# v loaded in fp32 and cast by GpSimd, two half sums moved to DMA, and a new order of steps, in a gated linear attention with a rational MLP

## The chip, the cores and the metric

One Trainium2 chip, one NeuronCore. The time is device microseconds of one execution; the number for a kernel is the median of its runs. The engines are TensorE (PE, with its weight loads as PEld), VectorE (DVE), ScalarE (ACT), GpSimd (POOL) and SyncE (SP, which here only issues DMAs).

## The reference

Inputs `q`, `k`, `v`, `f_logit` are fp32 of shape (4 batches, 8 heads, 768 tokens, 48); `w_in` is 384x2048, `w_out` 2048x384.

```
f = 1 / (1 + exp(-f_logit))
for t in tokens:                                  # per batch and head
    state = f[t][:, None] * state + outer(k[t], v[t])      # 48 x 48
    y[t]  = q[t] @ state
x = y as 3072 tokens x 384
h = x @ w_in
P = a0 + a1*h + a2*h^2 + a3*h^3
Q = 1 + |b0|*|h| + |b1|*h^2
out = (P / (Q + 1e-6)) @ w_out                    # fp32, 3072 x 384
```

## The kernel before, in words

**Units.** The work is cut into 12 units of 256 tokens: unit n is chunk n // 4 of batch n % 4, so units n and n + 4 share a state. Of a unit's 256 tokens partition p holds tokens 2p and 2p + 1, and the upper and lower 64 partitions are two blocks j of 128 tokens. All in a unit is one chain of steps, and each step is one function of the kernel that issues a few instructions:

- `ld` (line 193) loads f, k, q or v of the unit. f, k and q go through SP's queue as fp32 into tiles with three buffers each. v goes through POOL's queue, whose DMA casts it to bf16, also with three buffers.
- `ef`, `ls` (271, 276, ACT) make log(1 + exp(-f)); `cs` (286, PE) sums it along the tokens; `A` (302, ACT) are the exponentials; `xa` (308, DVE) multiplies k (`xa n 1`) and q (`xa n 0`) by them; `T` (320, PE) transposes and `Te` (330, 332) copies out.
- `sc` (345, PE) makes the scores, `mk` (353, DVE) multiplies them by the causal mask into `scm`. `kv` (414, PE) makes the new part of the state from k and **v**, `si` (425) adds the old state, `ae`, `st` (441, 445) scale it.
- `yi`, `yb` (367, PE) sum y from the old state and from scores times v. A head is 48 wide and PE writes y in pieces of 32, so a pair of heads makes three pieces: the first and last read **v** as loaded; the middle one, which lies across both heads, reads `vmp`, a tile that `vm` (360, POOL) fills with two copies of 16 columns per pair of heads: two POOL instructions of 128 elements per partition in each unit.
- `ye` (435, 436) copies y out as xT. `h` (454; `ha`, `hb` 478) multiplies by w_in in four pieces of four 128-column blocks; `hy` (484, ACT) copies out.
- The rational function: `sq` (489) makes h^2, `ab` (497) |h|; Q is summed by PE (`u`, 505), by DVE (`zv`, 515) or by an accumulating DMA from POOL's queue (`zd`, 519); ACT makes 1/Q as exp(-ln Q) (`ln` 510, `lz` 523, `ex` 527). `p1` (531), `pm` (545), `p2` (536) make the two halves of P on DVE, which are summed by DVE (`tv`, 553) or by an accumulating DMA (`ta`, 549); `gm` (557, DVE) multiplies by 1/Q. A **half sum** is `zv`, `zd`, `tv` or `ta` on 8 of the 16 blocks (2048 elements per partition).
- `o` (567, PE) multiplies by w_out, `oe` (574) copies out, `so` (580) stores.
- `wi` (199) and `wo` (205) load w_in and w_out in four parts each by POOL's queue with a cast. `dz` (295) are matmuls that only keep PE busy.

**Order.** The text `ORDER` lists 823 steps, and each engine runs its own instructions in the order in which the steps stand there (`tc.manual_schedule()`); waits between engines follow from the data and the buffers. So the order of two steps matters when they share an engine or a DMA queue. `>ls.1` behind a step makes it wait for that other step, `@2` names the PSUM slot. PSUM has four slots that all steps share.

Of the kernel before, what the change touches and what calls it, by code (L numbers as in the profile page):

```python
# [8 lines left out]
F32 = mybir.dt.float32  # L9
# [10 lines left out]
ld 0 f 2 4; cu 1; cz 0; ab_ b a; ld 0 f 0 2; cz 2; ld 0 k 0 2; cu 0; ld 0 k 2 4; ld 0 q 2 4; ci; cm; dz 9 @0  # L20
ld 0 q 0 2; ld 1 f; ld 0 v; ab_ a s; ld 1 k; fa; ld 1 q; ef 0 2 4; ef 0 0 2; cz 3; ls 0 0 2; ls 0 2 4; cz 1
cs 0 2 4 @2; cs 0 0 2 @3; A 0 0 2 4; dz 4 @0; A 0 1 2 4; xa 0 0 2 4; A 0 1 0 2; xa 0 1 2 4; A 0 0 0 2
xa 0 1 0 2; T 0 2 4 @0; vm 0 1; kv 0 @3; Te 0 2 4; wi 8 12; xa 0 0 0 2; ae 0; sc 0 1 @0; si 0 0; mk 0 1
T 0 0 2 @2; ef 1; dz 5 @1; fr; Te 0 0 2; ld 2 f >mk.0.1; ls 1; ld 3 f; st 0 0; sc 0 0 @0; ld 2 k; cs 1 @2
wi 12 16 >ls.1; mk 0 0; ld 2 q; ld 3 k; yi 0 1 @1; vm 0 0; A 1 1; ld 1 v; ld 3 q; yb 0 2 4; yb 0 0 2; A 1 0
si 0 1; wi 4 8; ye 0 0 1 v; ye 0 1 3 s; xa 1 1; wi 0 4; h 0 8 12 @1; xa 1 0; ld 2 v; fb; T 1 @0; hy 0 8 12 v
Te 1 s; st 0 1; ab 0 8 12; ha 0 12 16 @0; ef 2; sc 1 1 @3; sc 1 0 @1; mk 1 1; ls 2; hb 0 12 16; cs 2 @2; ld 5 f
sq 0 8 12; hy 0 12 16; ld 4 f; mk 1 0; kv 1 @3; vm 1 1; ld 4 q; vm 1 0; A 2 1; si 1 0; dz 1 @0; ae 1; A 2 0
yb 1 0 2 @1; st 1 0; yb 1 2 4; sq 0 12 16; yi 1 1; si 1 1; p1 0 8 16; ye 1 s; h 0 4 8 @2; ab 0 12 16; ef 3
pm 0 8 16; h 1 12 16 @1; ls 3; st 1 1; hy 0 4 8; p2 0 8 16; h 1 8 12 @0; hy 1 12 16; ab 0 4 8; sq 0 4 8  # L30
h 0 0 4 @2; hy 1 8 12; xa 2 1; ab 1 8 16; h 1 4 8 @3; ld 5 k; hy 0 0 4; ld 4 k; sq 1 8 16; ld 6 f; cs 3 @1
# [12 lines left out]
h 3 4 8 @1; ef 7; pm 2 0 16; hy 3 8 12; o 0 1 4 8; hy 3 4 8; sc 4 1 @0; o 0 1 0 4; ls 6; mk 4 1; ta 2 8 16
sc 4 0 @1; ex 1 0 8; o 0 0 0 4; ld 9 f; xa 5 0; cs 6 @0; mk 4 0; o 0 0 4 8; A 6 1; o 0 0 12 16; st 4 0; A 6 0
yb 4 0 2 @1; ab 3 0 16; yb 4 2 4; oe 0 0 2 s; yi 4 0; yi 4 1; si 4 1; sq 3 0 16; ye 4 s; T 5 @2; ef 8
u 2 0 4 @1; Te 5 s; h 4 4 8 @0; st 4 1; zd 3 8 16; ln 2 0 4; gm 1 8 16; h 4 12 16 @2; lz 2 8 16; p1 3 0 16
sc 5 0 @3; h 4 0 4 @1; xa 6 0; hy 4 4 8; vm 6 1; ta 2 0 8; gm 1 0 8; hy 4 12 16; ld 9 q; h 4 8 12 @0; vm 5 0
ld 7 k; ld 7 v; hy 4 0 4; mk 5 0; vm 6 0; u 2 4 8 @2; zd 3 0 8; hy 4 8 12; pm 3 0 16; o 1 1 4 8 @1; ln 2 4 8
o 1 0 0 4; ex 2 8 16; sc 5 1 @2; kv 5 @0; mk 5 1; yi 5 0 @3; yb 5 0 2; ls 7; o 1 0 12 16; sq 4 0 16; o 1 0 4 8  # L50
ex 2 0 8; ld 10 f; cs 7 @2; ld 7 q; si 5 0; o 1 1 12 16; p2 3 0 16; ae 5; A 7 0; o 1 0 8 12; lz 3 8 16
o 1 1 0 4; st 5 0; ta 3 0 8; xa 6 1; si 5 1; yi 5 1; yb 5 2 4; st 5 1; A 7 1; o 1 1 8 12; ab 4 0 16; ye 5 s
T 6 @0; ef 9; p1 4 0 16; zd 4 0 8; kv 6 @2; Te 6 s; h 5 4 8 @3; gm 2 0 16; ae 6; ls 8; h 5 8 12 @0; hy 5 4 8
oe 1 0 2 s; p2 4 0 16; h 5 0 4 @3; vm 7 1; ta 3 8 16; hy 5 8 12; zd 4 8 16; xa 7 1; ef 10; sc 6 1 @1; si 6 0
h 5 12 16 @0; ld 8 v; mk 6 1; hy 5 0 4; ld 10 k; ld 9 k; ld 8 q; lz 3 0 8; st 6 0; sc 6 0 @1; ld 11 f; xa 7 0
# [9 lines left out]
ld 11 k; ld 10 q; hy 7 8 12; gm 4 0 16; vm 8 0; vm 8 1; ld 10 v; T 8 @2; ae 8; hy 7 4 8; ta 5 0 8; h 7 0 4 @3
ls 10; st 8 0; zd 6 8 16; Te 8 s; p1 6 0 16; o 4 0 12 16 @1; zd 6 0 8; hy 7 0 4; sc 8 0 @2; kv 9 @0; xa 9 0
lz 5 0 8; sc 8 1 @3; mk 8 0; o 4 0 0 4; o 4 0 8 12; mk 8 1; ls 11; o 4 0 4 8; si 9 0; ae 9; ex 5 8 16
h 7 12 16 @2; p2 6 0 16; st 9 0; o 4 1 4 8; hy 7 12 16; pm 6 0 16; yi 8 1 @3; yi 8 0; yb 8 2 4; ex 5 0 8
# [38 lines left out]
def kernel(  # L107
# [64 lines left out]
    def unit(n):  # L172
        if n not in units:
            c, b = divmod(n, B)
            units[n] = dict(c=c, b=b, qk=qkp[n % 2], ls=lsp[n % 2], vm=vmp[n % 2], st=states[b])
        return units[n]
# [449 lines left out]
```

## Time and profile before

| | |
|---|---|
| median of 3 runs | 216.9 us (216.26 to 217.07) |
| span of the profiled execution, first to last instruction | 214.4 us, 2.5 us less than the median |
| PE busy | 201.0 us (94%) |
| DVE busy | 201.7 us (94%), 213 instructions |
| ACT busy | 195.8 us (91%) |
| POOL busy | 83.7 us (39%) |
| DMA | 43.20 MB, mean 202 GB/s |

An engine's busy time is the time that at least one of its instructions ran. Instructions of one engine overlap a little at their ends (a DVE row of 1.21 us is followed 1.13 us after its start), and matmuls are pipelined, so a busy PE is not at its peak. POOL's DMA issues count as POOL's busy time, SP's don't.

### The profile page before, as it was taken

The page shows a single profiled execution, that of the slowest core. Times are in us where ns is not written, and L with a number is a line of the kernel's source. Part 1 is how long each engine was busy: PE and PEld are TensorE (multiplying, and loading weights), DVE is VectorE, ACT ScalarE, POOL GpSimd, SP SyncE. Part 2 cuts the span into 40 slices and gives each one's busy share as a digit, 9 for nine tenths or more (in the row PEclk, how much of TensorE's full clock was granted, in tenths as well). Part 3 has the DMA queues.
Part 4 walks back from the last instruction along what each step waited for, and adds up shares of the span by engine and source line. Part 5 has one row for each costly group of instructions (what it writes and reads, how often), then busy time and mean ns, then how long its engine had stood idle before and what let it go on. Part 6 is the DMA issues. An engine that isn't in the chain of part 4 may idle for free.

```text
span 214.4 us, 7128 instructions
## 1 busy us (share of the span) xinstructions
PE 201.0 (94%) x3166; PEld 139.9 (65%) x3166; DVE 201.7 (94%) x213; ACT 195.8 (91%) x204; POOL 83.7 (39%) x93
## 2 busy tenths in 40 slices
PE   5875999899999999999999899999999999999993
PEld 1544587567767686586687587686577676776461
DVE  4786899999999999999999999999999999999991
ACT  3574689999999999999999999999999999999990
POOL 5161009009165072183270496696350603114200
PEclk9999999999999999999999999999999999999999
DMA  5999999999999999999999499999499896988823
GB/s 143 240 257 217 201 242 197 195 223 223 187 200 248 247 235 219 253 228 203 192 292 193 81 294 215 209 225 208 89 192 200 164 196 126 174 282 151 187 84 148
DMA packets 61199, 43.20 MB, mean 202 GB/s; under 512 B 51184, under 2 KB 55024, under 8 KB 61168
## 3 DMA queue, kind: packets, MB, share of 16 engines
q0 software_dynamic: 21520, 23.86, 67.3%
q1 hardware_dynamic: 39360, 18.68, 34.5%
q8 instruction: 25, 0.41, 0.8%
q10 hardware_dynamic: 288, 0.20, 0.3%
q14 instruction: 6, 0.05, 0.1%
HBM read 25.17 MB, written 4.72 MB: 139 GB/s over the span
## 4 chain that ended last, share of the span: by engine, by line
PE 39%; DVE 29%; ACT 14%; DMA 9%; issue 6%; SPq 2%; POOL 1%; DVEq 0%
PE hp L454 13%; PE op L567 12%; DVE gall L557 6%; DMA w_in_sb<-in_moe_w_in_dram 6%; DVE gall L545 4%; ACT qi L527 4%; ACT hy L484 4%; DVE z L497 3%; DVE h L489 3%; DVE scm L353 3%; DMA fn<-in_f_logit_dram 3%; PE u L505 3%; DVE gall L531 3%; PE y L367 2%; DVE hy L536 2%
## 5 line engine op out<-in xcount | busy, mean ns | idle before, releaser
L567 PE MATMUL op<-w_out_sb,gall 128*128 128x384 bf16 x384 | 69.2, 326 | 0.4 <-DVE gall L557 0.4
L454 PE MATMUL hp<-xT,w_in_sb 128*128 128x256 bf16 x564 | 66.7, 273 | 2.1 <-DMA w_in_sb<-in_moe_w_in_dram 2.0
L454 PEld LDWEIGHTS <-w_in_sb 128*128 128x128 bf16 x564 | 54.2, 98 | 11.5 <-DMA w_in_sb<-in_moe_w_in_dram 2.5
L567 PEld LDWEIGHTS <-gall 128*128 128x128 bf16 x384 | 36.1, 98 | 23.6 <-DVE gall L557 0.8
L484 ACT CAST hy<-hp 128x1024 bf16<-128x1024 f32 x47 | 48.1, 1076 | 2.3 <-PE hp L478 1.4
L527 ACT ACTIVATE qi<-lq 128x2048 bf16<-128x2048 f32 (+1 forms) x26 | 48.0, 1861 | 0.1
L360 POOL COPY vmp<-vn 128x128 bf16<-128x128 bf16 x24 | 35.2, 1516 | 28.4 <-DMA vn<-in_v_dram 22.7
L549 POOL DMA_DIRECT2D gall<-hy x20 | 20.0, 1068 | 53.9 <-ACT lsp L276 10.6
L523 ACT ACTIVATE lq<-z 128x2048 f32<-128x2048 bf16 (+1 forms) x20 | 36.8, 1874 | 0.0
L353 DVE TENSOR_TENSOR scm<-sc,mask 128x1024 bf16<-128x1024 f32 x24 | 29.0, 1215 | 1.9 <-PE sc L345 1.7
L489 DVE TENSOR_TENSOR h<-hy 128x4096 bf16<-128x4096 bf16 (+2 forms) x19 | 28.5, 1500 | 0.0
L557 DVE TENSOR_TENSOR gall<-gall,qi 128x4096 bf16<-128x4096 bf16 (+2 forms) x17 | 28.2, 1666 | 0.2
L545 DVE TENSOR_TENSOR gall<-gall,h 128x4096 bf16<-128x4096 bf16 (+2 forms) x17 | 28.1, 1652 | 0.0
L519 POOL DMA_DIRECT2D z<-h x17 | 19.3, 1366 | 17.0 <-PE u L505 6.0
L302 ACT ACTIVATE A<-cs 128x768 f32<-128x768 f32 (+1 forms) x26 | 19.4, 799 | 1.8 <-PE cs L286 1.8
L193 POOL DMA_DIRECT2D vn<-in_v_dram x12 | 12.4, 1030 | 15.7 <-PE y L367 7.9
L531 DVE TENSOR_SCALAR gall<-hy,a_sb 128x4096 bf16<-128x4096 bf16 (+1 forms) x14 | 16.9, 1208 | 0.0
L536 DVE TENSOR_SCALAR hy<-hy,a_sb 128x4096 bf16<-128x4096 bf16 (+1 forms) x14 | 16.6, 1185 | 0.0
L497 DVE TENSOR_SCALAR z<-hy 128x4096 uint16<-128x4096 uint16 (+2 forms) x19 | 15.7, 834 | 0.4 <-ACT hy L484 0.4
L330 ACT COPY qkT<-tp 128x1024 f32<-128x1024 f32 x11 | 11.6, 1058 | 3.2 <-PE tp L320 3.2
L320 PE MATMUL tp<-ident,qkp 128*128 128x128 bf16 x192 | 12.9, 219 | 0.8 <-DVE qkp L308 0.5
L320 PEld LDWEIGHTS <-qkp 128*128 128x128 bf16 x192 | 11.5, 98 | 2.5 <-DVE qkp L308 0.9
(73 smaller groups left out, 255.8 us busy)
## 6 DMA issues: line engine op xcount, KB each, us to landing
gall<-hy POOLq DMA_DIRECT2D x18, 512.0 KB, 7.1
z<-h POOLq DMA_DIRECT2D x15, 512.0 KB, 8.4
fn<-in_f_logit_dram SPq DMA_DIRECT2D x11, 384.0 KB, 8.5
kn<-in_k_dram SPq DMA_DIRECT2D x11, 384.0 KB, 12.1
qn<-in_q_dram SPq DMA_DIRECT2D x11, 384.0 KB, 11.3
out_dram<-osb SPq DMA_DIRECT2D x11, 384.0 KB, 5.1
vn<-in_v_dram POOLq DMA_DIRECT2D x12, 192.0 KB, 8.9
w_in_sb<-in_moe_w_in_dram POOLq DMA_DIRECT2D x4, 384.0 KB, 10.1
```

Of the source, the lines that this page charges most:

```text
L320: nc.tensor.transpose(t[:, x, i, p, :], s["qk"][:, i, x, 2 * p:2 * p + 2, :].rearrange("t h d -> t (h d)"), ident)
L353: return nc.vector.tensor_mul(t, s["sc", g].rearrange("s r a i t -> s (r a) (i t)"), mb)
L360: nc.gpsimd.tensor_copy(s["vm"][:, :, :, 32 * x:32 * x + 16], src)
L454: nc.tensor.matmul(t[:, m - m0, :], w_in_sb[:, kk, m * P:(m + 1) * P], s["x"][:, kk].rearrange("p i j t -> p (i j t)"), start=(kk == 0), s ...
L484: (nc.scalar.copy if eng == "s" else nc.vector.tensor_copy)(fl(big(s, "hy", "hy", 3), m0, m1), fl(s["hp", m0], 0, m1 - m0))
L489: return nc.vector.tensor_mul(fl(big(s, "h2", "h2", 2), m0, m1), fl(s["hy"], m0, m1), fl(s["hy"], m0, m1))
L523: nc.scalar.activation(fl(lq, m0, m1), fl(s["z"], m0, m1), AF.Ln, scale=regs[2], bias=1.0 + 1e-6)
L527: nc.scalar.activation(fl(qi, m0, m1), fl(lq, m0, m1), AF.Exp, scale=-1.0)
L531: return nc.vector.tensor_scalar(fl(big(s, "g", "gall", 3), m0, m1), fl(s["hy"], m0, m1), a_sb[:, 3:4], a_sb[:, 2:3], op0=ALU.mult, op1=AL ...
L545: return nc.vector.tensor_mul(fl(s["g"], m0, m1), fl(s["g"], m0, m1), fl(s["h2"], m0, m1))
L557: return nc.vector.tensor_mul(fl(s["g"], m0, m1), fl(s["g"], m0, m1), fl(qi, m0, m1))
L567: nc.tensor.matmul(s["op", j][:, j, 0:DM], s["g"][:, m, P * j:P * j + P], w_out_sb[:, m, :], start=(s["on", j] == 1), stop=(s["on", j] == KF))
```

## The change

**v.** v is loaded as fp32 through SP's queue, into a tile with one buffer in place of three. `vc` replaces `vm`: two POOL instructions per unit (one for the even heads, one for the odd) cast all of v to bf16 into `vpd`, where each head has 64 columns and the odd heads start at column 16; the rest is zero. Each cast has 384 elements per partition. Both the middle pieces and all other readers of v (`yb`, `kv`) now read `vpd`, so `kv` waits for the casts too. The next unit's load of v waits for both casts.

**mask** is bf16 in place of fp32. **Two half sums** (`zv 5 8 16` and `tv 4 8 16`) become `zd 5 8 16` and `ta 4 8 16`, that is DMAs from POOL's queue. **The order** of all 823 steps is new. The number of matmuls and of ACT's and DVE's other large instructions stays.

```diff
-ld 0 f 2 4; cu 1; cz 0; ab_ b a; ld 0 f 0 2; cz 2; ld 0 k 0 2; cu 0; ld 0 k 2 4; ld 0 q 2 4; ci; cm; dz 9 @0
+ab_ b a; ld 0 f 2 4; ef 0 2 4; cz 0; cu 0; cu 1; ld 0 f 0 2; fa; ls 0 2 4; cz 3; ld 0 k 0 2; ld 0 q 2 4
...
-    mask = consts.tile([P, 2, 2, R], F32, name="mask")
+    mask = consts.tile([P, 2, 2, R], BF16, name="mask")
...
-    vmp = [consts.tile([P, 2, HP, 48], BF16, name=f"vmp{i}") for i in range(2)]
+    vpd = [consts.tile([P, HP, 2, 2, E], BF16, name=f"vpd{i}") for i in range(2)]
...
-        eng = nc.gpsimd if what == "v" else nc.sync
         if what not in s:
-            s[what] = ld.tile([P, H, 2, D], BF16 if what == "v" else F32, name=what + "n")
+            s[what] = ld.tile([P, H, 2, D], F32, name=what + "n", bufs=1 if what == "v" else 3)
         hh = slice(2 * a0, 2 * a1)
-        i = eng.dma_start(out=s[what][:, hh].rearrange("p h i d -> p h (i d)"),
+        i = nc.sync.dma_start(out=s[what][:, hh].rearrange("p h i d -> p h (i d)"),
...
-            nc.vector.memset(vmp[i][:, :, :, 16:32], 0.0)
+            nc.vector.memset(vpd[i][:, :, 0, :, D:E], 0.0)
+            nc.vector.memset(vpd[i][:, :, 1, :, 0:E - D], 0.0)
...
-    def vm(n, x):
-        s = unit(n)
-        vv = s["v"].rearrange("p (a r) i d -> p r i a d", r=2)
-        src = vv[:, 0, :, :, 32:48] if x == 0 else vv[:, 1, :, :, 0:16]
-        nc.gpsimd.tensor_copy(s["vm"][:, :, :, 32 * x:32 * x + 16], src)
+    def vc(n, par, *args):
+        s = unit(n)
+        hold = [x[1:] for x in args if x.startswith(">")]
+        copy = nc.scalar.copy if "s" in args else (nc.vector if "v" in args else nc.gpsimd).tensor_copy
+        i = copy(s["vp"][:, :, par, :, 16 * par:16 * par + D],
+                 s["v"].rearrange("p (a r) i d -> p r a i d", r=2)[:, par])
...
-                        if kk == 1:
-                            w = s["vm"][r, i0, a, 16 * par:16 * par + 32]
-                        else:
-                            w = s["v"][r, 2 * a + par, i0, 16 * par:16 * par + 32]
+                        e = 32 * (kk - par)
+                        w = s["vp"][r, a, par, i0, e:e + 32]
...
-                                         s["qk"][r, i, 1, 2 * a + par, :], s["v"][r, 2 * a + par, i, :],
+                                         s["qk"][r, i, 1, 2 * a + par, :], s["vp"][r, a, par, i, 16 * par:16 * par + D],
```

In the new order no `vc` uses its options, so all 24 casts are POOL's.

**POOL's queue at the start**, behind the constants; `vn` is a unit's v, `vmp0` and `vmp1` serve even and odd units. Before:

```order
L193 DMA vn_158<-in_v_dram 128x8x96
L360 COPY vmp0_94<-vn_158 128x8x16
L199 DMA w_in_sb_110<-in_moe_w_in_dram 128x3x512 x2
L360 COPY vmp0_94<-vn_158 128x8x16
L193 DMA vn_355<-in_v_dram 128x8x96
L199 DMA w_in_sb_110<-in_moe_w_in_dram 128x3x512 x2
L193 DMA vn_445<-in_v_dram 128x8x96
L360 COPY vmp1_95<-vn_355 128x8x16 x2
```

Now, with `vpd0` and `vpd1` in their place:

```order
L358 CAST vpd0_94<-vn_166 128x4x2x48 x2
L197 DMA w_in_sb_110<-in_moe_w_in_dram 128x3x512 x3
L358 CAST vpd1_95<-vn_293 128x4x2x48 x2
L197 DMA w_in_sb_110<-in_moe_w_in_dram 128x3x512
L358 CAST vpd0_94<-vn_650 128x4x2x48 x2
L358 CAST vpd1_95<-vn_732 128x4x2x48
L548 DMA gall_689<-hy_463 128x2048
```

The first part of w_in stands behind both casts of unit 0, three parts follow one another, and the fourth stands behind the casts of unit 1. No load of v is left in this queue.

**SP's queue** from the loads of unit 1 on (`fn`, `kn`, `qn` are a unit's f, k and q). Before:

```order
L193 DMA kn<-in_k_dram 128x8x96
L193 DMA qn<-in_q_dram 128x8x96
L193 DMA fn<-in_f_logit_dram 128x8x96 x2
L193 DMA kn<-in_k_dram 128x8x96
L193 DMA qn<-in_q_dram 128x8x96
```

Now:

```order
L191 DMA qn<-in_q_dram 128x8x96
L191 DMA kn<-in_k_dram 128x8x96
L191 DMA vn<-in_v_dram 128x8x96
L191 DMA fn<-in_f_logit_dram 128x8x96 x2
L191 DMA vn<-in_v_dram 128x8x96
L191 DMA kn<-in_k_dram 128x8x96
L191 DMA qn<-in_q_dram 128x8x96
```

The loads of k and q of unit 2 (the last two rows of both) now stand behind the v of unit 1 and the v of unit 2, and the latter waits until both casts of unit 1 are done.

**DVE at the two half sums**, in the middle of the kernel. Before:

```order
L353 TENSOR_TENSOR scm_2385<-sc,mask 128x1024
L531 TENSOR_SCALAR gall<-hy,a_sb 128x4096
L553 TENSOR_TENSOR gall<-gall,hy 128x2048
L515 TENSOR_TENSOR z<-z,h_2283 128x2048
L353 TENSOR_TENSOR scm_2477<-sc,mask 128x1024
L545 TENSOR_TENSOR gall<-gall,h_2283 128x4096
```

Now, from the instructions on that make what the two half sums add (`z` and `h_2228` of unit 5; `gall` with `h_2003`, and `hy` on line 535, of unit 4):

```order
L496 TENSOR_SCALAR z<-hy 128x4096
L444 TENSOR_TENSOR state_1_101<-sv,alast 128x384
L488 TENSOR_TENSOR h_2228<-hy 128x4096
L544 TENSOR_TENSOR gall<-gall,h_2003 128x4096
L444 TENSOR_TENSOR state_0_100<-sv,alast 128x384
L352 TENSOR_TENSOR scm_2331<-sc,mask 128x1024
L556 TENSOR_TENSOR gall<-gall,qi 128x4096
L535 TENSOR_SCALAR hy<-hy,a_sb 128x4096
L307 TENSOR_TENSOR qkp_87<-qn,A 128x2x8x48
```

The rows of the two half sums (2048 elements each) are gone from DVE; the neighbours are those of the new order.

More of the change, by code (lines that the diff above doesn't have):

```diff
@@ L65 @@
[L65 to L68, printed above, removed]
-yb 8 0 2; cs 10 @0; ld 11 v; o 4 1 0 4; sq 7 0 16; A 10 1; o 4 1 12 16; ye 8 s; o 4 1 8 12; A 10 0; T 9 @3
```

155 lines of the change are left out of this document (81 added, 74 removed).

## The prediction

> **What bounds the kernel now.** I read the page's busy times first, then the busy time by stage, then the chain of waits.
>
> ```profile
> span 214.4 us, 7128 instructions
> PE 201.0 (94%) x3166; PEld 139.9 (65%) x3166; DVE 201.7 (94%) x213; ACT 195.8 (91%) x204; POOL 83.7 (39%) x93
> ```
>
> ```profile
> core 0: us, PE busy (x) PEld busy (x) DVE busy (x) ACT busy (x) POOL busy (x), PEclk, DMA share, GB/s
> 0.00:22.00 22.00, 14.95 (x256) 8.88 (x260) 14.96 (x44) 11.48 (x18) 8.48 (x21) 1.00 1.15 214
> 22.00:35.00 13.00, 12.50 (x222) 9.59 (x211) 12.32 (x17) 10.36 (x13) 2.85 (x5) 1.00 1.16 220
> 35.00:100.00 65.00, 63.91 (x1108) 45.42 (x1106) 65.00 (x61) 64.89 (x74) 27.80 (x30) 1.00 1.19 221
> 100.00:205.00 105.00, 103.54 (x1566) 72.57 (x1565) 104.94 (x86) 104.80 (x96) 44.57 (x38) 1.00 0.96 195
> 205.00:214.40 9.40, 6.09 (x38) 3.42 (x35) 4.46 (x8) 4.23 (x5) 0.00 (x0) 1.00 0.23 86
> ```
>
> The second view says nearly all. From 35 to 205 us DVE and ACT are busy without a break, and PE within 1.5%. DVE is idle for 7.0 us before 22, 0.7 until 35, 0.1 until 205 and 4.9 at the end. The granted clock is 1.00 throughout. So there are a head in which DVE waits for loads and for PE, a middle in which a microsecond more on DVE or ACT is a microsecond more in the span, and a tail.
>
> The chain agrees: in time order it is a DMA, then PE, then ACT, then DVE.
>
> ```profile
> 14.72 12.03 DMA w_in_sb<-in_moe_w_in_dram
> 26.79 4.12 PE hp L454 x36
> ...
> 100.82 3.61 ACT qi L527 x2
> ...
> 153.99 2.23 DVE gall L557
> ```
>
> A consequence for gains: taking 2 us off DVE alone shortens the span by 2 us at most, and by less if ACT, which has the same middle, doesn't end earlier too. A loss on DVE isn't damped so.
>
> **The change part by part.**
>
> *Two half sums leave DVE.*
>
> ```profile
> L553 DVE TENSOR_TENSOR gall<-gall,hy 128x2048 bf16<-128x2048 bf16 x4 | 4.9, 1216 | 0.0
> L515 DVE TENSOR_TENSOR z<-z,h 128x2048 bf16<-128x2048 bf16 x2 | 2.4, 1212 | 0.0
> ```
>
> One of each goes: 1.22 + 1.21, so **-2.4 us** of DVE. What they become costs POOL two issues and the DMA engines two transfers:
>
> ```profile
> gall<-hy POOLq DMA_DIRECT2D x18, 512.0 KB, 7.1
> z<-h POOLq DMA_DIRECT2D x15, 512.0 KB, 8.4
> ```
>
> Between the instructions that make the operands of the two sums and `gm 4` and `lz 5`, which read them, stand 12 and 22 us of DVE work in the new order (the rows' durations added up), more than issue and landing: no cost.
>
> *v through SP's queue, and 24 casts on POOL in place of 24 copies.* SP isn't counted as busy, and POOL has 130 us to spare, so neither queue's own time matters. What matters is what a POOL instruction does to DVE. The old copies:
>
> ```profile
> L360 POOL COPY vmp<-vn 128x128 bf16<-128x128 bf16 x24 | 35.2, 1516 | 28.4 <-DMA vn<-in_v_dram 22.7 <-PE y L367 5.2 <-issue 0.5
> ```
>
> ```profile
> 9.40 0.28 POOL L360 COPY vmp<-vn 128x128 bf16<-128x128 bf16 x1 [5.23 <-DMA vn<-in_v_dram]
> ...
> 136.91 2.31 POOL L360 COPY vmp<-vn 128x128 bf16<-128x128 bf16 x1
> ```
>
> ```profile
> 135.91 2.28 DVE L489 TENSOR_TENSOR h<-hy 128x4096 bf16<-128x4096 bf16 x1
> 138.12 0.95 DVE L308 TENSOR_TENSOR qkp<-kn,A 128x768 bf16<-128x768 f32 x1
> 139.12 0.96 DVE L308 TENSOR_TENSOR qkp<-qn,A 128x768 bf16<-128x768 f32 x1
> ```
>
> The same copy takes 0.28 us at 9.40, beside an idle stretch of DVE, and 2.31 at 136.91, where it lasts through two DVE instructions and ends at 139.22, just behind the second (139.07). The DVE instruction behind starts at 139.12. Two lines up, the start is 138.12 against an end of 138.19, an overlap of 0.07; here there is a gap of 0.05. So POOL mostly waits, and DVE loses about 0.12 us at the copy's end. [...]
>
> The trace has no such cast. By the nearest rows:
>
> ```profile
> masks.py:197 POOL MEMSET ident<- 128x128 bf16 x1 | 0.2, 204 | 0.0
> L610 POOL MEMSET const-bfloat16-1.0<- 128x1 bf16 x1 | 0.1, 101 | 0.0
> masks.py:199 POOL TENSOR_SCALAR_AFFINE_SELECT ident<-ident 128x128 bf16<-128x128 bf16 x1 | 0.3, 330 | 0.1
> ```
>
> 127 more elements cost a memset 103 ns, 0.8 ns each; an instruction that also reads costs at most (330 - 101) / 127 = 1.8. The cast has 384 elements in place of 128, so 256 x 0.8 to 1.8 = 0.21 to 0.46 us more, 0.49 to 0.74 in all. [...] Two groups read a single SBUF tensor beside PSUM:
>
> ```profile
> L353 DVE TENSOR_TENSOR scm<-sc,mask 128x1024 bf16<-128x1024 f32 x24 | 29.0, 1215 | 1.9 <-PE sc L345 1.7
> L445 DVE TENSOR_TENSOR state<-sv,alast 128x384 bf16<-128x384 f32 x20 | 10.9, 547 | 0.2 <-ACT alast L441 0.2
> ```
>
> They are 39.9 of DVE's 201.7 us. [...] I take three casts in four (18, about DVE's share of other instructions) at 0.21, the memset's price, which is the better bound because the copy of 128 elements took 0.28 and not 0.33: **+3.8 us**.
>
> *mask in bf16, memsets, moved constants.* `scm` has an fp32 input from PSUM as before and stays at its 1.2 us; the extra memsets lie in DVE's idle 7 us of the head. Nothing; if the head were full, 0.2.
>
> *The head.* Two effects of opposite sign.
>
> ```profile
> 22.09 1.23 DVE L353 TENSOR_TENSOR scm<-sc,mask 128x1024 bf16<-128x1024 f32 x1 [1.74 <-PE sc L345]
> ...
> 30.68 0.95 DVE L308 TENSOR_TENSOR qkp<-kn,A 128x768 bf16<-128x768 f32 x1
> ...
> 34.16 0.94 DVE L308 TENSOR_TENSOR qkp<-qn,A 128x768 bf16<-128x768 f32 x1
> ```
>
> At 22.09 DVE has waited 1.74 us for scores of unit 1, which PE could make only after the second part of w_in. Now `kv 1` and `sc 1 0` stand ahead of that part, and v of unit 1 is issued right behind unit 1's q and k: up to 1.7 won. Against it: k and q of unit 2 are issued behind two more loads of v, and the second of these waits for the casts of unit 1.
>
> ```profile
> DMA to landing us min/median/max: 13.9/13.9/13.9
> ```
>
> ```profile
> DMA to landing us min/median/max: 14.2/14.2/14.2
> ```
>
> These are k and q of unit 2 before, issued at 12.95 and 16.46: landed at 26.9 and 30.7, read by DVE at 30.68 and 34.16, 3.8 and 3.5 us later. Two loads of 384 KB at the 220 GB/s of the second stage are 2 x 1.8 = 3.6 us, and the new order reads k 1.0 and q 2.5 us sooner (DVE's instructions ahead of them by their rows, old order less new), on top of the up to 1.7 won: 1 to 4 late. [...] I set gain and loss equal: **0**, bounds -1.7 and +2.5.
>
> *The tail.* The half sums of unit 11 land after 3.8 and 3.3 us, behind an issue on POOL of 0.84:
>
> ```profile
> z<-h POOLq DMA_DIRECT2D x2, 256.0 KB, 3.8
> gall<-hy POOLq DMA_DIRECT2D x2, 256.0 KB, 3.3
> ```
>
> ```profile
> 201.12 0.84 POOL L549 DMA_DIRECT2D gall<-hy  x1 [2.53 <-DVE z L497]
> ```
>
> For the first of z the new order leaves 3.8 us of DVE work until ACT's turn to read it, the old one 5.9; needed are 3.8 + 0.84 = 4.6. **+0.5**, bounds 0 and +1.5.
>
> Sum on the profiled execution: 214.4 - 2.4 + 3.8 + 0 + 0.5 = 216.3. The median lay 2.5 above the span, so 218.8.
>
> **The rivals.**
>
> 1. *Faster: DVE loses nothing to the casts.* [...] Then -2.4 stays, with the head's -1.4 (1.74 less a rest): 216.9 - 3.8 = **213.1**. For it: POOL was the one that waited. It decides if a cast costs DVE under 0.1 us. Against it: ACT must gain as much, and its work is unchanged.
> 2. *Slower by more: v's one buffer becomes a chain.* Each load of v waits for the last casts, the casts for POOL's turn between DVE's instructions, and SP's next k, q and f wait behind the load. Here:
>
> ```profile
> 60.74 4.63 POOL L360 COPY vmp<-vn 128x128 bf16<-128x128 bf16 x1 [2.45 <-DMA vn<-in_v_dram]
> ```
>
> ```profile
> 44.85 0.44 PE L414 MATMUL sv<-vn,qkp 64*64 64x48 bf16 x32
> ```
>
> ```profile
> DMA to landing us min/median/max: 5.5/8.9/16.3
> ```
>
> A load of v takes 8.9 us, up to 16.3, and one copy 4.63. Unit 3's v is the fourth in the chain: unit 1's lands at about 17, casts to 19, unit 2's 10 to 16 later, casts, unit 3's 9 more, casts: 40 to 48, and `kv 3` ran at 44.85. Up to 3 late there, and PE's queue with it: 218.8 + 3 = **221.8**. Behind `kv 3` stand 20 us of DVE work until `kv 4`, more than one load with its casts, so the chain would be caught up.
> 3. *Nothing that counts.* The casts eat what the half sums gave, all within 1 us: **216.9**.
>
> **How the numbers follow.** 0.5% is 1.1 us, about what a measurement of this kernel can tell from no change. The forecast (casts cost DVE 3 to 7) has 0.40, rival 1 has 0.34, rival 2 has 0.16, rival 3 has 0.10. The forecast's lower edge lies within 0.5% (0.05), so faster 0.34, same 0.15, slower 0.51. Predicted: 218.8. The range goes from 212.0 (rival 1 with the head's full 1.7 and half a microsecond of scatter) to 223.0 (rival 2 with the tail's bound).
>
> **What would show it.** Line 358's casts at 0.5 to 0.7 us where DVE is idle; DVE's busy time up although it has two instructions fewer, with two-input instructions starting late behind a cast: the +3.8. If DVE's busy time falls to 199 and its idle stays near 12.7, rival 1. If DVE or PE wait for casts or for v, k or q between 25 and 60 us, rival 2. I would be wrong altogether if the new order opened waits between ACT, PE and DVE in the middle, where there are now none.

## The result, and the profile after

| | before | after |
|---|---|---|
| median | 216.7 us (216.26 to 217.07, 4 runs) | **223.4 us** (222.83 to 224.18, 4 runs) |
| ratio | | 1.031, 95% interval 1.028 to 1.035 |
| profiled execution: span, own time | 214.4 us | 222.5 us, 224.2 |
| DVE busy, idle | 201.7, 12.7 us | 203.3, 19.2 us |

The change makes the kernel 6.7 us slower. The direction was forecast, with a chance of 0.51, the size not: 218.8 was predicted, with a range up to 223.0. In the runs further down a median counts every execution, a ratio leaves out those more than 1.5% above the fastest of their kernel (one each of e3, f4 and g2, two of h1).

The page of the changed kernel, in its busy times, then the busy time by the stages that the prediction used (the last stage now ends at 222.5):

```profile
span 222.5 us, 7138 instructions
...
PE 205.9 (93%) x3159; PEld 140.8 (63%) x3166; DVE 203.3 (91%) x213; ACT 196.2 (88%) x204; POOL 62.4 (28%) x83
```

```profile
0.00:22.00 22.00, 16.18 (x281) 9.64 (x281) 15.79 (x47) 10.89 (x18) 7.60 (x20) 1.00 1.07 222
22.00:35.00 13.00, 12.03 (x177) 9.34 (x179) 10.40 (x15) 9.97 (x14) 1.47 (x2) 1.00 1.07 241
35.00:100.00 65.00, 62.09 (x1031) 43.28 (x1037) 62.68 (x58) 62.20 (x70) 19.19 (x23) 0.97 1.07 218
100.00:205.00 105.00, 102.56 (x1615) 71.72 (x1604) 103.17 (x79) 102.33 (x93) 32.34 (x38) 1.00 0.97 209
205.00:222.50 17.50, 13.04 (x75) 6.83 (x74) 11.23 (x18) 10.81 (x13) 1.76 (x2) 1.00 0.47 143
```

The columns are stage, length, then busy time of PE, PEld, DVE, ACT and POOL, the granted clock, the DMA share and GB/s. Length less DVE's busy time is DVE's idle time. Up to 35 us it is 8.8 us (before 7.7), from 35 to 205 it is 4.15 (before 0.06), behind 205 it is 6.3 (before 4.9). ACT too now stands still for 5.5 us of the middle; before it was 0.3. That is the failure in one view: **the middle, where DVE never waited, has gaps.** The 8.1 us between the two spans are 1.6 more work on DVE, 1.1 more idle time in the head, 4.1 in the middle and 1.3 at the end.

What ended the larger gaps of DVE from 35 us on (start, length, instruction, and in brackets the idle time before it and its releaser; the wait of 1.6 us for the last output block, 1.2 before, is left out):

```profile
49.50 0.56 DVE L444 TENSOR_TENSOR state<-sv,alast 128x384 bf16<-128x384 f32 x1 [1.05 <-PE sv L424]
67.59 1.22 DVE L352 TENSOR_TENSOR scm<-sc,mask 128x1024 bf16<-128x1024 f32 x1 [0.67 <-PE sc L344]
69.04 1.23 DVE L352 TENSOR_TENSOR scm<-sc,mask 128x1024 bf16<-128x1024 f32 x1 [0.23 <-PE sc L344]
82.66 1.23 DVE L352 TENSOR_TENSOR scm<-sc,mask 128x1024 bf16<-128x1024 f32 x1 [0.29 <-PE sc L344]
128.65 2.29 DVE L556 TENSOR_TENSOR gall<-gall,qi 128x4096 bf16<-128x4096 bf16 x1 [1.53 <-DMA gall<-hy]
211.12 1.29 DVE L556 TENSOR_TENSOR gall<-gall,qi 128x1024 bf16<-128x1024 bf16 x2 [0.66 <-DMA gall<-hy]
```

Three waits for scores, one for the state, and two for a half sum that a DMA makes. The one at 128.65 is `gm 4`, and its half sum is `ta 4 8 16`, one of the two that the change moved to DMA; nothing waited for the other, `zd 5 8 16`, which landed at 118.59. The chain of waits shows how late `ta 4 8 16` was:

```profile
115.55 0.54 POOL gall L548
116.09 12.44 DMA gall<-hy
```

**What a cast costs.** Unhindered it took 0.5 us (501 ns for the shortest of the 24), as estimated. What DVE lost differed with what the cast lay over and with which of the two was at work first, as these rows show. Two casts over a mask product, which reads PSUM (POOL's rows, then DVE's):

```profile
110.62 0.96 POOL L358 CAST vpd<-vn 128x384 bf16<-128x384 f32 x2 [0.38 <-DMA vn<-in_v_dram]
```

```profile
110.59 1.21 DVE L352 TENSOR_TENSOR scm<-sc,mask 128x1024 bf16<-128x1024 f32 x1
111.72 2.27 DVE L556 TENSOR_TENSOR gall<-gall,qi 128x4096 bf16<-128x4096 bf16 x1
```

Neither side loses anything: the product took 1.21 us and the two casts 0.96 together. A DMA issue and two casts on POOL, and `p1`, which has one 16-bit input in SBUF and a constant and begins when POOL is at work already:

```profile
149.68 0.84 POOL L518 DMA_DIRECT2D z<-h  x1 [8.69 <-PE sc L344]
150.22 1.25 POOL L358 CAST vpd<-vn 128x384 bf16<-128x384 f32 x2
```

```profile
149.93 2.76 DVE L530 TENSOR_SCALAR gall<-hy,a_sb 128x4096 bf16<-128x4096 bf16 x1
152.61 1.21 DVE L352 TENSOR_TENSOR scm<-sc,mask 128x1024 bf16<-128x1024 f32 x1
```

`p1` takes 2.76 us in place of 1.34, 0.7 more per cast. It ends 1.22 us behind the second cast's end (151.47), so about its own length behind it, as if it had waited for POOL and then run. The other rows fit this reading: `p1` at 101.38 ends 1.10 behind a cast's end, `p1` at 165.20 1.20, and |h| at 39.21, which takes 0.68 alone, 0.56. A cast's row of 0.8 us isn't a cast that shares with DVE: it begins 0.3 us ahead of the end of the DMA issue before it, and in the run f3 such a cast took 0.84 us at 65.60, when DVE was idle. Where DVE was at work first, the cast waited, and took 2.82 us:

```profile
97.86 2.82 POOL L358 CAST vpd<-vn 128x384 bf16<-128x384 f32 x1
```

It began inside a product of two SBUF tensors, lasted through the whole one behind it (98.04 to 100.32), ended 0.37 us after that and cost DVE nothing. The cast that began at 83.44, 0.36 us ahead of such a product, made the product 0.3 us longer. The groups show the sum: the ten large `p1` go from 13.4 (before) to 15.9 us, the mask products stay at 1215 ns with the mask in bf16.

```profile
L530 DVE TENSOR_SCALAR gall<-hy,a_sb 128x4096 bf16<-128x4096 bf16 x10 | 15.9, 1585 | 0.2 <-PE op L566 0.2
...
L352 DVE TENSOR_TENSOR scm<-sc,mask 128x1024 bf16<-128x1024 f32 x24 | 29.0, 1215 | 2.8 <-PE sc L344 2.7
```

DVE's work, less the two half sums, is 203.3 + 2.4 - 201.7 = 4.0 us more than with the old copies; the prediction had 3.8.

### The profile page after: what moved, and what is told of

Its sections match the earlier page's. It is cut to its first block, busy times and chain, and to the rows that moved or that the text cites. A ratio compares the mean times of both kernels' runs of the same rounds, so it can differ in the third digit from the quotient of the medians.

```text
span 222.5 us, 7138 instructions
## 1 busy us (share of the span) xinstructions
PE 205.9 (93%) x3159; PEld 140.8 (63%) x3166; DVE 203.3 (91%) x213; ACT 196.2 (88%) x204; POOL 62.4 (28%) x83
## 4 chain that ended last, share of the span: by engine, by line
DVE 39%; PE 27%; DMA 18%; issue 8%; ACT 5%; POOL 0%; SPq 0%; DVEq 0%; ACTq 0%; POOLq 0%
DMA gall<-hy 11%; PE op L566 7%; DVE gall L556 7%; DMA fn<-in_f_logit_dram 7%; PE hp L453 7%; DVE scm L352 6%; DVE gall L544 6%; DVE h L488 4%; DVE gall L530 4%; DVE hy L535 4%; PE u L504 3%; DVE z L496 3%; PE y L368 3%; DVE qkp L307 3%; PE tp L319 2%
## 5 line engine op out<-in xcount | busy, mean ns | idle before, releaser
L483 ACT CAST hy<-hp 128x1024 bf16<-128x1024 f32 x47 | 47.1, 1045 | 3.2 <-PE hp L477 2.2
L526 ACT ACTIVATE qi<-lq 128x2048 bf16<-128x2048 f32 (+1 forms) x26 | 46.3, 1805 | 0.9 <-DVE gall L556 0.8
L548 POOL DMA_DIRECT2D gall<-hy x21 | 22.6, 1172 | 53.4 <-ACT xT L435 16.5
L522 ACT ACTIVATE lq<-z 128x2048 f32<-128x2048 bf16 (+1 forms) x20 | 35.9, 1806 | 0.2 <-DMA z<-h 0.2
L358 POOL CAST vpd<-vn 128x384 bf16<-128x384 f32 x24 | 22.1, 951 | 42.5 <-DMA vn<-in_v_dram 27.1
L352 DVE TENSOR_TENSOR scm<-sc,mask 128x1024 bf16<-128x1024 f32 x24 | 29.0, 1215 | 2.8 <-PE sc L344 2.7
L518 POOL DMA_DIRECT2D z<-h x18 | 17.7, 1005 | 46.0 <-PE hp L453 12.3
L530 DVE TENSOR_SCALAR gall<-hy,a_sb 128x4096 bf16<-128x4096 bf16 (+1 forms) x14 | 19.1, 1363 | 0.2 <-PE op L566 0.2
L496 DVE TENSOR_SCALAR z<-hy 128x4096 uint16<-128x4096 uint16 (+2 forms) x19 | 16.3, 872 | 0.0
L270 ACT ACTIVATE fn<-fn 128x768 f32<-128x768 f32 (+1 forms) x13 | 10.5, 823 | 5.3 <-DMA fn<-in_f_logit_dram 5.3
L329 ACT COPY qkT<-tp 128x1024 f32<-128x1024 f32 x11 | 11.4, 1038 | 2.4 <-PE tp L319 2.4
L509 ACT ACTIVATE lq<-u 128x1024 f32<-128x1024 f32 x11 | 11.5, 1050 | 2.1 <-PE u L504 2.1
L319 PE MATMUL tp<-ident,qkp 128*128 128x128 bf16 x192 | 12.7, 219 | 0.1
```

The source lines that it names most:

```text
L352: return nc.vector.tensor_mul(t, s["sc", g].rearrange("s r a i t -> s (r a) (i t)"), mb)
L483: (nc.scalar.copy if eng == "s" else nc.vector.tensor_copy)(fl(big(s, "hy", "hy", 3), m0, m1), fl(s["hp", m0], 0, m1 - m0))
L496: return nc.vector.tensor_scalar(fl(big(s, "z", "z", 2), m0, m1).bitcast(U16), fl(s["hy"], m0, m1).bitcast(U16), 0x7FFF, None, op0=ALU.bit ...
L522: nc.scalar.activation(fl(lq, m0, m1), fl(s["z"], m0, m1), AF.Ln, scale=regs[2], bias=1.0 + 1e-6)
L526: nc.scalar.activation(fl(qi, m0, m1), fl(lq, m0, m1), AF.Exp, scale=-1.0)
L530: return nc.vector.tensor_scalar(fl(big(s, "g", "gall", 3), m0, m1), fl(s["hy"], m0, m1), a_sb[:, 3:4], a_sb[:, 2:3], op0=ALU.mult, op1=AL ...
```

## The experiments

My theory after the result: DVE's work is as forecast, and what was not forecast is that the new order, which is right only if every duration is the one it was made for, has waits of its own. The rivals: the waits come from the new way of v (its one buffer, SP's queue, the casts), or from a few places that can be mended.

| run | edit | median us | ratio to before, 95% interval |
|---|---|---|---|
| e1_new_order_old_v | new order, v as before | 228.4 | 1.048 to 1.060 |
| e4_old_order_new_v | old order, v's new way | 227.0 | 1.046 to 1.056 |
| h1_old_order_new_v_placed | the same, placed with care | 229.1 | 1.052 to 1.062 |
| e2_new_halves_on_dve | new order, two half sums on DVE | 225.1 | 1.036 to 1.044 |
| e3_old_halves_by_dma | old order, two half sums by DMA | 217.8 | 1.004 to 1.010 |
| h2_old_plus_24_casts | kernel before and 24 casts | 224.4 | 1.030 to 1.042 |
| g2_tiny_casts | new, casts cut to 1 of 48 columns | 223.4 | 1.024 to 1.039 |
| f1_no_casts | new, 20 casts left out | 229.6 | 1.059 to 1.063 |
| f2_one_cast_later | new, one cast held | 222.3 | 1.025 to 1.037 |
| f3_casts_under_fp32 | new, five casts held | 223.2 | 1.028 to 1.035 |
| f4_w_in_not_held | new, w_in's last quarter early | 222.9 | 1.027 to 1.032 |
| g1_warm_on_free_slot | new, filler in a free slot | 223.5 | 1.025 to 1.036 |
| g3_three_mends | new, f2 + f4 + g1 | 222.5 | 1.025 to 1.031 |
| g4_mends_tiny_casts | g3 and tiny casts | 222.2 | 1.024 to 1.030 |
| i1_casts_and_scores_moved | new, three units' casts held, scores earlier | 221.7 | 1.016 to 1.029 |

The kernel before had medians of 216.05 to 216.7 beside them.

### Order and way of v, crossed

```diff
 e1, on the changed kernel (v's load, mask, kv and yb as before)
-vc 0 0; vc 0 1
+vm 0 0; vm 0 1
 e4 and h1, on the changed kernel: ORDER of before with vm out, vc in, ld n v behind vc n-1
```

> The changed kernel's order of steps with v on its old way: v as bf16 by the cast-DMA of GpSimd's queue with three buffers, each cast replaced at its place by the old 128-element copy. Theory (the loss is split: some 4.4 us on VectorE where casts lie over its fast 16-bit instructions, of which the old copies took 1.7, and some 6 us of waits that the new order of steps opened): the casts' part goes, the waits stay, 219.5 to 221.5 us. Rival (the fp32 load on SP's queue with its one buffer makes the waits too): 215 to 217.5 us. Rival (the order alone, the casts cost nothing): 223 us.

> The kernel before with its order of steps and its half sums on VectorE, and the new way of v alone: fp32 by SP's queue with one buffer, the 24 casts about where the old copies stood (v's loads and the casts moved as far as the one buffer and the state sum need it), mask in bf16. Theory (the casts cost VectorE some 4.4 us less the 1.7 that the old copies cost): 219 to 221 us. Rival (v's way makes the waits too): 223 us or more. Rival (the order alone): 216.5 to 217.5 us.

> The order of before with the new way of v once more, placed with more care: v0 loaded ahead of q's second half; both casts of a unit together some four microseconds of work ahead of the state sum that reads them, each load of v right behind the casts of the unit before it, so that no cast waits long for its load with half sums queued behind it. Theory (order and way of v were searched together, and each fits only the other; the way of v alone then costs its casts and the waits that its one buffer makes in a full order): 219 to 224 us. Rival (the first placing was merely bad, and the way of v costs little): 216 to 218.5 us.

Both crossings are slower than either kernel: 228.4 for the new order with the old v, above all three expectations, and 227.0 for the old order with the new v, as the rival of "223 or more" had it. Placing v's loads and casts with more care made it 229.1, not less, above both expectations. If order and way of v had prices that add up, the losses of e1 and e4, 11.6 and 11.0 us, would together be about the change's 6.7. They aren't: in the places tried (one for e1, two for the other) **each order fits its own way of v alone**, and the runs don't tell the order's share of the loss from that of the way of v. In e1 a wait can be followed. A copy of v stood in POOL's queue waiting for its load, and a half sum behind it:

```profile
76.71 1.80 POOL L361 COPY vmp<-vn 128x128 bf16<-128x128 bf16 x1 [7.64 <-DMA vn<-in_v_dram]
78.46 1.29 POOL L550 DMA_DIRECT2D gall<-hy  x1
```

```profile
83.58 1.93 ACT L485 CAST hy<-hp 128x1024 bf16<-128x1024 f32 x2 [2.63 <-DMA gall<-hy]
```

ACT waited 2.6 us for the transfer of this half sum (it reads a tile that ACT's copy is to write, so ACT has to wait), and DVE behind it 2.2, at 85.11. In e4 it is the same with casts:

```profile
163.62 0.51 POOL L359 CAST vpd<-vn 128x384 bf16<-128x384 f32 x1 [11.41 <-DMA vn<-in_v_dram]
164.22 0.84 POOL L519 DMA_DIRECT2D z<-h  x1
164.76 2.90 POOL L549 DMA_DIRECT2D gall<-hy  x2
165.83 2.70 POOL L519 DMA_DIRECT2D z<-h  x1
```

ACT waited 2.9 us, until 177.97, for the second `z<-h`, issued at 165.83. In these two places the way of v is tied to the order through POOL's queue; that all of the 11 us come so isn't shown.

### The half sums

```diff
 e2, on the changed kernel        e3, on the kernel before: the reverse
-zd 5 8 16
+zv 5 8 16
-ta 4 8 16
+tv 4 8 16
```

> The changed kernel with only its two half sums of units 4 and 5 back on VectorE. Theory: VectorE gets 2.4 us of work back, and of the waits only the one of 1.5 us before the product of unit 4 goes, so 223.5 to 225 us. Rival (the two transfers load the DMA engines and GpSimd's queue and so make more of the waits): under 222.5 us.

> The kernel before with only the two half sums of units 4 and 5 by DMA, order and v as before. Theory (VectorE is the bound of the middle together with TensorE and ScalarE): VectorE loses 2.4 us of work; with nothing late behind it 214.3 us. Rival (a half sum by DMA comes late for the product, or TensorE and ScalarE, just as full, hold the time): 216 to 218 us.

In the new order putting both back on DVE costs (1.040 - 1.031) x 216.5 = 1.9 us (the intervals just don't overlap); the theory's 223.5 to 225 was missed by 0.1. So there they seem to be worth 1.9 of their 2.4. In the old order the same edit does not gain 2.4, it **loses** 1.5 (interval 0.8 to 2.1). 2.4 us less work on DVE, in the stage where DVE never waits, made the kernel slower. The only profile of e3 is of its slowest execution (220.2 us), so it shows places and not sizes. From 35 to 100 us DVE still never waits; from 100 to 205, where the two sums are, it is idle for 3.7 us, before 0.06. It waits 1.90 us for scores at 115.69, and ACT waits for one of the two moved half sums, `zd 5 8 16`:

```profile
127.36 1.91 ACT L523 ACTIVATE lq<-z 128x2048 f32<-128x2048 bf16 x1 [1.55 <-DMA z<-h]
```

### What casts cost

```diff
 h2, on the kernel before, in vm
         nc.gpsimd.tensor_copy(s["vm"][:, :, :, 32 * x:32 * x + 16], src)
+        nc.gpsimd.tensor_copy(xo.rearrange("p (c w) -> p c w", w=8), _at(xi, [[0, 48], [1, 8]]))
 g2, on the changed kernel, in vc
+        w = D if n < 2 else 1
-        i = copy(s["vp"][:, :, par, :, 16 * par:16 * par + D],
-                 s["v"].rearrange("p (a r) i d -> p r a i d", r=2)[:, par])
+        i = copy(s["vp"][:, :, par, :, 16 * par:16 * par + w],
+                 s["v"].rearrange("p (a r) i d -> p r a i d", r=2)[:, par, :, :, 0:w])
 f1, on the changed kernel: vc n 0 and vc n 1 left out for n >= 2
```

(The constant of h2's casts is 8 columns wide and read 48 times over. "The first of their 16 columns" in the expectation below is a slip: a head has 48 columns, and the cast kept the first.)

> The kernel before with 24 casts added, one behind each of its copies of v on GpSimd: 384 elements from fp32 to bf16, out of a constant of its own and into a tile that nobody reads, so that only their time beside VectorE counts. Theory (VectorE has no idle time from 35 to 205 us, so what casts take from it lengthens the run): a cast that falls on 16-bit instructions as often as in the changed kernel takes 4.4 us in all, 219.5 to 222 us. Rival (ScalarE and TensorE are as full, and VectorE's loss lies beside their work): 216.5 to 218 us.

> The changed kernel with the 20 casts of units 2 to 11 cut to the first of their 16 columns: every cast keeps its place and its waits and GpSimd's queue its pace, only its time beside VectorE is nearly gone; the other columns of the padded v keep older values, so the outputs are not the reference's. Theory (the casts cost VectorE some 4 us, and TensorE's stall at 40 us hangs on one of them): 218 to 220.5 us. Rival (the time taken from VectorE is given back in waits for TensorE, as when five casts were moved): 221.5 to 223.5 us.

> The changed kernel without the 20 casts of units 2 to 11; v is still loaded, and the units from 2 on use the padded v of units 0 and 1, so their outputs are not the reference's. Theory (the casts that lie over VectorE's 16-bit instructions lengthen them by 4.4 us in the profile, and the one at 39 us also starves TensorE, whose clock then halves for 3.4 us): 217 to 219.5 us. Rival (the loss is the new order's waits, whatever the casts do): 221.5 to 223.5 us.

h2 measures casts by themselves, in the order whose middle is full: **+7.8 us** (interval 6.5 to 9.1), above the theory's 219.5 to 222. DVE's busy time rises from 201.7 to 206.7, 5.0 us or 0.21 per cast, and its idle time from 12.7 to 16.3. Waits come on top, the first for a copy that stood behind a cast in POOL's queue (the cast ended at 57.63, the copy at 58.59):

```profile
58.64 0.24 PE L372 MATMUL y<-scm,vmp 64*32 64x128 bf16 x4 [1.95 <-POOL vmp L364]
```

```profile
61.39 0.81 ACT L441 ACTIVATE xT<-y 128x768 bf16<-128x768 f32 x1 [2.88 <-PE y L372]
...
178.15 1.91 ACT L528 ACTIVATE lq<-z 128x2048 f32<-128x2048 bf16 x1 [2.25 <-DMA z<-h]
```

PE waits 1.95 us for a copy of v, ACT 2.88 for PE; at 178 ACT waits 2.25 for a half sum. So in the profile, 8.6 us longer than before, 5.0 us are time that DVE lost beside casts, and 3.6 are more idle time, 3.0 of it between 35 and 205 us. h2 also shows DVE waiting for a whole cast, which the prediction had in no row: the product at 58.36 took 1.76 us in place of 1.21 and ended 1.08 behind the end of a cast of 0.50 that stood behind a copy in POOL's queue.

In the changed kernel the reverse gives back next to nothing. With casts of one column (g2) DVE's busy time falls by 3.1 to 200.1. Its four runs took 222.0, 222.1, 224.6 and 228.7, so by itself g2 is not firm (its interval leaves 1.6 us either way). The pair g3 and g4 has narrow runs and differs in the casts alone: 222.45 and 222.20, no difference within about 0.9 us. Between their profiles DVE's busy time falls from 203.5 to 200.2, and its idle time rises from 16.8 to 19.7: of 3.3 us of work taken away 2.9 turn into waits. g2's stages:

```profile
35.00:100.00 65.00, 62.99 (x1080) 44.31 (x1079) 62.58 (x60) 63.49 (x71) 17.74 (x25) 1.00 1.09 223
100.00:205.00 105.00, 103.03 (x1569) 71.52 (x1568) 101.77 (x79) 102.99 (x96) 28.25 (x35) 1.00 0.96 208
```

DVE's idle time in the middle is now 5.65 us, against 4.15 with whole casts. One of the new waits:

```profile
162.00 1.23 DVE L352 TENSOR_TENSOR scm<-sc,mask 128x1024 bf16<-128x1024 f32 x1 [1.65 <-PE sc L344]
```

With whole casts `p1` of unit 8 at 165 and that of unit 7 at 150 were 2.1 us longer, and no wait for scores stood there. f1, 20 casts left out, was 6 us slower than the changed kernel, and misses both expectations: casts also pace POOL's queue. Without them the four parts of w_out were issued at 31.5 to 33.7 us (in the changed kernel at 39.9 to 53.6), and DVE waited for a q:

```profile
53.59 0.96 DVE L307 TENSOR_TENSOR qkp<-qn,A 128x768 bf16<-128x768 f32 x1 [9.71 <-DMA qn<-in_q_dram]
```

That load was issued at 38.8 and took 14.8 us. That w_out's early transfers made it late is argued from the times, not tried.

### Casts moved, and waits mended

```diff
-vc 3 0
+vc 3 0 >ab.1.8.16                  # f2, f3, g3, g4, i1
-vc 10 1; ... vc 11 1
+vc 10 1 >p1.7.0.16; ... vc 11 1 >p1.8.0.16      # f3, i1; f3 also vc 6 1 >p2.3.0.16, vc 7 1 >p1.4.0.16
-wi 12 16 >ls.1
+wi 12 16                           # f4, g3, g4
-dz 5 @3
+dz 5 @2                            # g1, g3, g4
-h 9 0 4 @1; o 5 0 4 8; sc 10 1 @2
+sc 10 1 @2; h 9 0 4 @1; o 5 0 4 8  # i1
```

> The changed kernel with one cast held: that of unit 3's even heads, which lay over the absolute value of unit 1 at 39.4 us and made it 0.9 us longer, starts behind that instruction, under the mask product that follows. Theory (one cast, 0.9 us on VectorE, then TensorE idle for 1.9 us, its clock halved for 3.4 us, and ScalarE waiting 2.1 us for it): 220.5 to 222 us. Rival (the stall at 40 us has another cause, and only the 0.9 us go): 222.3 to 223.5 us.

> The changed kernel with five casts held (and so the casts behind them in GpSimd's queue), each behind the 16-bit instruction that it lay over, so that it runs under the mask product behind it, which reads PSUM in fp32 and did not grow in the profile: units 3, 6, 7, 10 and 11. Theory (which VectorE instruction a cast lies over sets its price): VectorE loses some 3.9 us of the 4.4 and the stall at 40 us goes, 217.5 to 220 us. Rival (the held casts make the half sums behind them in GpSimd's queue late, or the price moves to the mask product): 222 us or more.

> The changed kernel with the load of w_in's last quarter no longer held behind the logarithm of unit 1. Theory (TensorE waits 1.5 us for that quarter at 22.7 us, and ScalarE and VectorE behind it): 222 to 223 us. Rival (the quarter then shares the transfers with unit 1's q and v, whose cast and head come later): 224 us or more. Rival (the head's end is set elsewhere): 223.4 us as before.

f2 is one cast. In the changed kernel the chain around it reads:

```profile
38.96 1.83 DVE z L496 x2
40.80 1.15 DVE scm L352
41.98 1.28 PE y L368 x32
...
44.02 2.07 PE u L504 x6
```

The cast over the second `z`, which is |h|, costs 0.9 us, the mask product comes later by so much, and PE, which needs it, stands idle for 1.94 us before 41.98. Then the granted clock drops, and the stage reads 0.83 (first the changed kernel, then f2):

```profile
40.00:50.00 10.00, 7.79 (x155) 4.82 (x154) 8.95 (x12) 7.94 (x11) 2.61 (x4) 0.83 1.16 213
```

```profile
40.00:50.00 10.00, 8.90 (x188) 5.65 (x192) 10.00 (x13) 10.00 (x13) 3.33 (x5) 1.00 1.20 227
```

In f2 PE was idle for 0.99 us, the clock stayed at 1.00, ACT has 10.0 of 10 us in place of 7.94 and DVE 10.0 in place of 8.95. In that stage the theory fits. The median is 222.3, 1.2 below the changed kernel's, but one run of 224.5 leaves the ratio where it was (1.031): that the microsecond reached the end is not shown.

f3 takes the casts off `p1` (1342 ns in place of 1585), and the mask products under which they now run stay at 1218. That what a cast lies beside sets its price is shown for these. But DVE's busy time fell by 1.5 us only, to 201.8, and not by some 3.9: other casts now lay over other instructions (`p2` at 167.30 took 1.97 us in place of 1.33, the product at 86.61 1.60 in place of 1.22). And the time didn't follow: 223.2, the rival's. DVE now waited 1.57 us at 163.77 for scores, and GpSimd's half sums behind the held casts were late for ACT (0.93 us at 96.69).

f4 hit the theory's 222 to 223 with 222.9, but its interval can't tell it from the changed kernel. It decides nothing.

> The changed kernel with the five filler matmuls of the head in PSUM slot 2, which is free there, in place of slot 3, which they get only when ScalarE has read the sums in it. Theory (TensorE stands idle 1.1 us at 7.9 us for that slot, and in some executions its clock then stays at half for 3 to 14 us of the head): the filler starts at 7.9 us, the head is not slowed, 221 to 222.5 us, the runs nearer to each other. Rival (the head's end is set by w_in's quarters and unit 1's transfers): 223 to 224 us.

> The changed kernel with three edits together: the filler of the head in the free slot, the cast of unit 3's even heads behind the absolute value, w_in's last quarter not held. Theory (the three losses are apart from each other: clock in the head, stall at 40 us, wait for the quarter): 219 to 221 us. Rival (what one gives, the next wait takes): 222 to 223 us.

> The same three edits with the casts of units 2 to 11 cut to one column as well (outputs not the reference's). Theory (with head, stall and casts gone what is left of the new order is its late half sums, 2 us, against 2.4 us of half sums taken from VectorE): 215.5 to 217.5 us. Rival (the new order has waits of its own in the middle, which stay): 219 us or more.

> The changed kernel with the cast of unit 3 held as before, the casts of units 10 and 11 held so that they run under mask products (in the profiles this takes 2 us from two of VectorE's instructions), and the scores of unit 10's second half moved on TensorE ahead of a hidden block and an output block, since with the casts held VectorE waited 1.6 us for these scores at 164 us. Theory (the casts' time on VectorE does count, and was given back at that one wait): 220 to 221.3 us. Rival (each wait mended makes the next: the new order has no engine that is alone the bound): 222 to 223.5 us.

g1 gave nothing: 223.5, the rival's, and its clock dropped in the head all the same (from 14.0 to 17.4 us). g3 with all three came to 222.5, the rival's; f2's median alone was 222.3: the mends don't add up. g4, with tiny casts as well, came to 222.2, far from the 215.5 to 217.5 of the theory that the new order would then be as good as the old. So **5.8 us of the loss stay when the casts' time is gone and three waits are mended.** i1 took the wait for scores away from f3; 221.7 lies between theory and rival. The wait came back one instruction later:

```profile
161.36 1.22 DVE L354 TENSOR_TENSOR scm<-sc,mask 128x1024 bf16<-128x1024 f32 x1
163.68 1.35 DVE L532 TENSOR_SCALAR gall<-hy,a_sb 128x4096 bf16<-128x4096 bf16 x1 [1.10 <-PE op L568]
```

The scores were there at 161.4, and now the output block that they had passed on PE was late, whose buffer `p1` needs. i1 is the best version of the new order, 2.2% (4.8 us) behind the kernel before; no run beat that kernel.

## Why the prediction was wrong

Term by term, from the two profiled executions:

| term | predicted us | measured us |
|---|---|---|
| two half sums leave DVE | -2.4 | -2.4 on DVE |
| their transfers | 0 | +1.5 (the wait at 128.65) |
| casts, on DVE | +3.8 | +4.0 |
| head | 0 (-1.7 to +2.5) | +1.1 |
| waits between engines in the middle | 0 | +2.6 |
| tail | +0.5 (0 to 1.5) | +1.3 |
| sum | +1.9 | +8.1 |

**The step that failed** is the one named last in the prediction: that the middle stays without waits between ACT, PE and DVE. From "DVE and ACT are busy without a break" it followed that a microsecond of work is a microsecond of time. The prediction limited that for gains ("by 2 us at most"), and then took the gain in full; for losses it said that they are not damped, and did not ask whether they grow. What the runs showed in its place: DVE idles for 4.15 us of the middle, before 0.06, and a change of its work doesn't come out as a change of the time. 2.4 us less on DVE in the old order made it 1.5 slower (e3), 5.0 us more made it 7.8 slower (h2), and 3.3 us less in the new order gave 0.25 (g3 and g4). The busy shares before said that the old order was tight. They didn't say that the new one would be: that stood in no view of the old trace, and the prediction gave a new order of 823 steps no term of its own. Of the 4.1 us in the middle, 1.5 are the late half sum, 1.05 the state behind the drop of the clock, the rest waits for scores and small ones. What makes each is followed to its start for these two only (the transfer, the cast at 39.4); for the others, and for how much is the order's and how much the new way of v, it stays open.

**The half sums' transfers.** "12 us of DVE work, more than issue and landing: no cost" compared a sum of durations with a median landing of 7.1. This transfer took 12.4 from its issue, and 1.5 us of it showed. The trace before had the warning: its transfers into `gall` took up to 11.6 us and those into `z` up to 13.1, as much as the room.

**The casts.** The 0.5 us alone was right (501 ns measured, 0.49 to 0.74 foreseen). The loss on DVE, 4.0 for 3.8, was right by luck. The prediction charged 18 of 24 casts 0.21 us each, on every instruction that doesn't read PSUM, and expected two-input instructions to start late. That three casts in four cost DVE was the author's estimate, and no run shows it: in the trace most of the loss is three `p1` (2.5 us) and one |h| (0.9): one-input instructions that began while POOL was at work and lost 0.36 to 1.43 us each, while most casts lay over mask products (1215 ns, as before) or waited for DVE, as the one at 97.86, and cost it nothing. In the new order the loss hardly counts (g3 and g4); in the old order it counts more than in full (h2, where 24 casts cost DVE 0.21 us each).

**The rivals.** Rival 1 (DVE loses nothing) did not come: its sign was a busy time of 199. Nor did rival 2: POOL idled 27 us for v, but neither PE nor DVE waited for a cast or for v, k or q between 25 and 60 us. The gain of 1.7 in the head was not there either; DVE waited 1.2 us for unit 1's second scores at 23.73, and 0.8 at 31.12 for exponentials of an f whose load, behind a load of v in SP's queue, took from 14.38 to 26.48 (before, 12.37 to 21.58).

**The tail.** The prediction added the issue's 0.84 us to 3.8 us that the page counts from the issue on, so its 4.6 holds the issue twice. Of the measured 1.3, 0.66 is a wait for a half sum at 211.12; the rest is in smaller differences.

**Span and median.** The 2.5 us between them were 1.7 that lie between time and span in every execution on record (1.65 to 1.86: 224.2 against a span of 222.5; 216.05 against 214.4 in a later run of the kernel before) and 0.8 of scatter. That is why 8.1 us between the spans are 6.7 between the medians.

## What to carry to other kernels

Where three engines are full at once, their order is part of the kernel's durations: changing one duration, even downward, can open waits. The sum of the work removed and added bounds neither a loss nor a gain: here 5.0 us more cost 7.8 (h2), 2.4 more cost 1.9 (e2), 2.4 less cost 1.5 (e3). Forecast such a change with a wide range upward, take the longest transfer of the old trace and not the median, and look first in the new trace for idle time of the full engine, by stage. In this kernel GpSimd's casts cost VectorE nothing under the mask products, which read PSUM (1215 ns before and after), and most where they came ahead of a 16-bit `p1` (2.76 us in place of 1.34); but moving them didn't by itself gain time (f3), and what stood behind a waiting cast in GpSimd's queue came late too (in e4 a cast waited 11.4 us for its load, and ACT 2.9 for a half sum issued behind it).

## What the runs showed of the hardware

**TensorE's granted clock dropped for 3.41 us, or for two or three times that.** In the changed kernel's records it is at 0.50 from 41.8 to 45.2 us (3.413 us), behind 1.94 us of idle PE; in f1 a drop lasts 6.827 us, in e1 10.24. In g1, where PE was idle for the same 1.94 us, the stage from 40 to 50 us reads 0.83 too. The length of one idle stretch doesn't tell whether a drop follows: the clock stayed at 1.00 behind 1.46 us up to 22.72 in the changed kernel's trace and 0.99 us in f2, but also behind 1.90 us up to 21.08 in the kernel before. That the idle time made the drop is inferred. Of 40 timed executions of the kernel before, 22 had a mean clock of 0.997 or more, with a median of 216.05, and 18 a clock of 0.990 to 0.992, about one drop, with 216.7: a difference of about 0.7 us. In the changed kernel it doesn't show: three executions at 0.992 took 222.83, 223.08 and 224.18, the one at 1.000 took 223.80. In the head the same matmuls took different times in different executions. The five filler matmuls took 1.24 us in the changed kernel and 2.29 in e2, where nothing ahead of them differs; e2's clock records begin only at 21.4 us, so that this was the clock is inferred from the length:

```profile
9.02 1.24 PE L294 MATMUL warm<-Ui 128*128 128x512 bf16 x5 [1.14 <-ACT A L301]
```

```profile
9.03 2.29 PE L296 MATMUL warm<-Ui 128*128 128x512 bf16 x5 [1.09 <-ACT A L303]
```

**Casts and VectorE instructions waited for each other.** The trace has it on both sides. With DVE first the cast at 97.86 took 2.82 us, where the shortest took 0.50; with POOL first `p1` at 149.93 ended 1.22 us behind the casts' end, and `p1` at 101.38 1.10 behind, where it takes 1.33 alone. That each waited for the end of the other is read from these lengths. The mask products, which read one input from PSUM, stayed at 1.21 us.
